# Scores of a token tile as one scheduled step, with the row halves of the TensorE array in turn, in a banded attention and PReLU feed-forward kernel

## The chip, the cores and the metric

The kernel runs on one core of one Trainium2 chip. The metric is the device time of one execution in microseconds (us). Before the change it is 951.26 us, the median of three runs (951.15 to 951.86).

The engines are named as in the profile. PE is TensorE (matmuls, and PEld its weight loads), DVE is VectorE, ACT is ScalarE, POOL is GpSimd. SP is SyncE, whose queue issues most of the transfers.

## The reference

Attention over a causal band of 64 positions, for 8 sequences of 576 tokens with 8 heads of 64 elements, and then a feed-forward layer on all 4608 tokens (512 to 2048 to 512):

```python
scores = scale * np.matmul(q, k.transpose(0, 1, 3, 2))
mask = (rel >= 0) & (rel < window)              # rel = query position - key position, window = 64
scores = np.where(mask, scores, -1000000000.0)
scores = scores - np.max(scores, axis=-1, keepdims=True)
attn = np.exp(scores)
attn = attn / (np.sum(attn, axis=-1, keepdims=True) + 1e-09)
x = np.matmul(attn, v)                          # heads side by side: (4608, 512)
...
h = x @ w_in
g = np.maximum(h, 0.0) + alpha * np.minimum(h, 0.0)
return (g @ w_out).astype(np.float32)
```

q, k and v are float32. The two weight matrices arrive in eight bytes per element, and the kernel turns each into two parts, a high and a low one, of the type fp32r. Every product of the feed-forward layer is a sum of three matmuls of such parts.

## The kernel before, in words

**Tiling.** There are 36 tiles of 128 tokens, in 9 blocks of four. For each tile `attend` does the attention; for each block and each of the 16 slices f of the hidden layer `cell` does both matmul groups of the feed-forward layer. `weights(c)` fetches and converts one of 32 pieces of weights: piece 2f is the w_in slice of f, piece 2f + 1 the w_out slice.

**One tile's attention.** A tile is two windows of 64 queries (u = 0 and 1), each of which sees 128 keys. q and k lie with the 64 head elements along the partitions: window 0 in partitions 0 to 63, window 1 in partitions 64 to 127. A score matmul therefore uses a 64 by 64 piece of the array: its rows are given by u, its columns by which of two heads (h) it is for. Four pairs of heads (e) by two heads are 8 matmuls per window, and the scores of one window fill one PSUM bank. Each float32 matmul is two records in the trace. Behind the scores come a mask on DVE (L344, one per pair of heads and window), the exponential on ACT (L350), the norm (DVE L361 and L362, POOL L366), a transpose of the weights of attention (on PE, L383, for the first eight tiles; on DVE, L404, for the others), the values on PE (L419), and the split of the result into xh and xl (L423, L426).

**One cell.** 12 matmuls into `h` (L450), two passes of PReLU on ACT and DVE (L456, L459), a split into high and low parts (ACT L464, POOL or DVE L468), and 12 matmuls onto the four output banks `o` (L483).

**What sets the order.** Nothing is ordered at run time: each engine has one queue and works through it in order. The order is made beforehand, by the list scheduler `Plan`. Every piece of work is a `step` with the engines that may run it, how long it holds the engine and how long until its result is there, the steps it comes `after` (their results are needed) or `behind` (their start is enough), and the buffers it takes and gives back. `order` picks, again and again, the step that can start first, and among those that can start within 0.12 us of it the one with the earliest deadline. `deadlines` works these out backwards from the `want` times. A buffer is a name of a place in SBUF or a PSUM bank; of several free places other than the banks 4 to 7, the one that came free last is taken. Banks 4 to 7 go under the name "bank"; 0 to 3 are called "o" and belong to the output sums, and the first two tiles use them for scores and transposes.

**The steps around the change.** In `attend` the loads of a tile are two steps on SP, each the k of one window and two transfers of q, and one step for both transfers of v. The scores are two steps on PE, each `after` the load step of its own window and the second `behind` the first:

```python
sc = step({PE: (0.55, 0.65)}, score, [loads[u]], scores or behind, take=[sbk] + [wb] * (u == 0),
          give=[qb, kb])
```

A step whose transfer moves data is planned to land 1.3 us after its issue plus the time of its bytes behind those planned earlier, plus 1.5 us; there is no limit to how many are under way in the plan. In the program itself the transfers use eight semaphores in turn. From the second block on, a tile's loads are `behind` an earlier cell of the block before, and its scores `behind` a later one.

Of the kernel before, what the change touches and what calls it, by code (L numbers as in the profile page):

```python
# [9 lines left out]
F32 = mybir.dt.float32  # L10
# [4 lines left out]
ALU = mybir.AluOpType  # L15
# [6 lines left out]

HOP = 0.06
LOOK = 0.12


class Buffer:
# [15 lines left out]
class Plan:  # L43
# [15 lines left out]
    def deadlines(self):  # L59
        left = {id(s): len(s.before) for s in self.steps}  # L60
        todo = [s for s in self.steps if not s.before]
        while todo:
            s = todo.pop()
            lat = min(x[1] for x in s.engines.values()) + (3.0 + s.moved if s.moved else 0.0)
            s.late = min([s.want] + [b.late - (lat + HOP if s in b.after else 0.0) for b in s.before])
            for a in s.after + s.behind:
                left[id(a)] -= 1
                if not left[id(a)]:
                    todo.append(a)

    def order(self):
        self.deadlines()
        free = {e: 0.0 for e in (PE, DVE, ACT, POOL, SP)}
        lanes = 0.0
        left = {id(s): len(s.after) + len(s.behind) for s in self.steps}
        ready = [s for s in self.steps if not left[id(s)]]
        done = []
        while ready:
            best = None
            picks = {}  # L80
            for s in ready:
                t0 = max([0.0] + [a.end + HOP for a in s.after] + [a.start + 0.01 for a in s.behind])
                wants = {}
                for b in s.take:
                    wants[b.kind] = wants.get(b.kind, 0) + 1
                for kind, n in wants.items():
                    have = sorted(self.stock[kind])
                    t0 = max(t0, have[n - 1][0] + HOP if len(have) >= n else math.inf)
                if t0 == math.inf:
                    continue  # L90
                for e, (hold, lat) in s.engines.items():
                    picks.setdefault(e, []).append((max(t0, free[e]), s, e))
# [5 lines left out]
                    best = cost, x  # L98
            assert best, [s.late for s in ready]
            (_, (t, s, e)) = best  # L100

            hold, lat = s.engines[e]
            s.start, s.engine = t, e
            free[e] = t + hold
            s.end = t + lat
            if s.moved:
                lanes = max(lanes, t + hold + 1.3) + s.moved
                s.end = lanes + 1.5
            for b in s.take:
                have = self.stock[b.kind]  # L110
                have.sort()
# [28 lines left out]
def banded_attention_then_prelu_ffn(  # L140
# [11 lines left out]
    nc = tc.nc  # L152
    P = 128
# [138 lines left out]
    def attend(t, by_pe, want, loads_behind=(), behind=()):  # L292
        d = st[t]
        early = t < 2
        qb, kb, vb, wb, pb = Buffer("q", 2), Buffer("k", 2), Buffer("v", 1), Buffer("w", 2 if by_pe else 1), Buffer("pt", 1)
        loads = []
        for u in range(2):
            def load(_, u=u):
                if u == 0:
                    d["q"] = room(qb, [P, NP, 2, W], F32, f"q_{t}")  # L300
                    d["k"] = room(kb, [P, NP, 2, 2, W], F32, f"k_{t}")
                r = slice(u * D, (u + 1) * D)
                nc.sync.dma_start(d["k"][r].rearrange("d e b h w -> d e (b h w)"),
                                  kT[:, :, 2 * t + u:2 * t + u + 2].rearrange("e d b h w -> d e (b h w)"))
                for h in range(2):
                    (nc.scalar if t == 0 else nc.sync).dma_start(
                        d["q"][r, :, h, :], qT[:, :, t, h, u * W:(u + 1) * W].rearrange("e d q -> d e q"))
            loads.append(step({SP: (0.7 if t == 0 else 1.9, 1.9)}, load, (), loads_behind if u == 0 else loads[:1],
                              take=[qb, kb] if u == 0 else [], moved=2.1))

        def load_v(_):
            d["v"] = room(vb, [P, NP, 2, P], F32, f"v_{t}")
            for u in range(2):
# [4 lines left out]
        sums, scores = [], []  # L318
        for u in range(2):
            sbk = Buffer("o" if early else "bank", NP)  # L320

            def score(_, u=u, sbk=sbk):
                if u == 0:
                    d["w"] = room(wb, [P, NH, KW], F32, f"w_{t}")
                    d["nm"] = sb.tile([P, NH], F32, tag=f"nm{t % 2}", name=f"nm_{t}")
                    d["sm"] = sb.tile([P, NH], F32, tag=f"sm{t % 2}", name=f"sm_{t}")
                    d["rc"] = sb.tile([P, NH], F32, tag=f"rc{t % 2}", name=f"rc_{t}")
                d["s", u] = s = bank(sbk, [P, NP, KW], F32, f"s_{t}_{u}")
                r = slice(u * D, (u + 1) * D)
                for e in range(NP):  # L330
                    for h in range(2):
                        nc.tensor.matmul(s[h * W:(h + 1) * W, e], d["q"][r, e, h, :], d["k"][r, e, :, h, :],  # L332
                                         start=True, stop=True)
# [3 lines left out]
            scores = [sc]  # L337
            some = []
            for e in range(NP):
                g = u * NP + e  # L340

                def mask(_, u=u, e=e, g=g):
                    m = masks[:, 1 if (t * P + u * W) % seq == 0 else 0, :]
                    nc.vector.tensor_tensor_reduce(  # L344
                        out=d["w"][:, g, :], in0=d["s", u][:, e], in1=m, op0=ALU.add, op1=ALU.min,
                        scale=-SCALE, scalar=3.0e38, accum_out=d["nm"][:, g:g + 1])
# [6 lines left out]
                m = step({DVE: (0.21, 0.37)}, mask, [sc], give=[sbk])  # L353
                some.append(step({ACT: (0.385, 0.58)}, soft, [m]))
            sums.append(some)

# [16 lines left out]
        if by_pe:  # L373
            for u in range(2):
# [238 lines left out]
```

## Time and profile before

| | |
|---|---|
| median of three runs | 951.26 us (951.15 to 951.86) |
| profiled execution, its own time | 950.47 us |
| its span, first to last instruction | 948.8 us |
| granted TensorE clock, mean | 0.997 |
| PE busy | 923.4 us (97%) |
| DVE, ACT, POOL busy | 450.7, 387.0, 312.2 us |
| score matmuls (L332) | 1152 records, 66.3 us |
| value matmuls (L419) | 1152 records, 43.1 us |
| moved by DMA | 74.41 MB |

Busy time of PE counts each matmul until its modelled end, and successive matmuls overlap; so how long a group holds PE is read from its start to the start of the group behind it. In the rows of the time order, the first column is the start in us from the start of the span, the second how long the group of like instructions lasted, xN how many there are, and what stands in brackets is how long the engine was idle before and who ended that.

### The profile page before, as it was taken

To read this page: it belongs to the slowest core of one execution; us is meant where nothing else is said; L and a number is where in the kernel's file an instruction comes from. 1 tells how busy PE (TensorE), PEld (TensorE's weight loads), DVE (VectorE), ACT (ScalarE), POOL (GpSimd) and SP (SyncE) were. 2 spreads that over 40 slices of the span, in tenths; PEclk is the share of its full clock that TensorE was granted. 3 is DMA by queue.
4 is the path that set the end of the run, shared out by engine and by line. 5 is a ranking of instruction groups with operands and counts; after the bars stand their busy time and mean duration, and the time that the engine had idled before them with its cause. 6 is when DMAs were issued, how large, how long until landed. Compare 5 with 4: busy or idle time off the path is not lost.

```text
span 948.8 us, 15478 instructions
## 1 busy us (share of the span) xinstructions
PE 923.4 (97%) x5872; PEld 748.5 (79%) x5872; DVE 450.7 (48%) x1310; ACT 387.0 (41%) x1025; POOL 312.2 (33%) x243
## 2 busy tenths in 40 slices
PE   5799999999999999999999999999999999999998
PEld 4578877888888888888888888888888888888886
DVE  2787995444444444445344534454444444441111
ACT  4777775333433333333433333342333343332222
POOL 2565675322222222222322322222222222232221
PEclk9999999999999999999999999999999999999999
DMA  9697665320432025201620151205220432001001
GB/s 202 163 234 183 178 198 124 87 57 1 101 92 55 23 57 132 56 23 34 156 56 23 35 128 51 56 19 136 58 56 1 92 98 57 23 1 45 1 1 44
DMA packets 96409, 74.41 MB, mean 78 GB/s; under 512 B 44624, under 2 KB 89680, under 8 KB 96336
## 3 DMA queue, kind: packets, MB, share of 16 engines
q1 hardware_dynamic: 93184, 73.16, 31.0%
q8 instruction: 46, 0.75, 0.3%
q10 hardware_dynamic: 3152, 0.27, 0.3%
q14 instruction: 27, 0.22, 0.1%
HBM read 63.97 MB, written 9.44 MB: 77 GB/s over the span
## 4 chain that ended last, share of the span: by engine, by line
PE 86%; issue 1%; DVE 1%; POOLq 0%; ACT 0%; POOL 0%; ACTq 0%
PE o L483 39%; PE h L450 38%; PE s L332 5%; PE av L419 3%; POOLq L609 0%; PE t L383 0%; DVE wout_l L275 0%; DVE g L459 0%; ACT g L456 0%; DVE two L239 0%; DVE os L519 0%; ACT gh L464 0%; DVE val L256 0%; DVE two L247 0%; DVE w L344 0%
## 5 line engine op out<-in xcount | busy, mean ns | idle before, releaser
L468 POOL TENSOR_TENSOR gl<-g,gh 128x512 fp32r<-128x512 f32 (+1 forms) x136 | 174.0, 1280 | 441.3 <-ACT gh L464 435.0
L459 DVE SCALAR_TENSOR_TENSOR g<-h,s_sb,g 128x512 f32<-128x512 f32 (+1 forms) x148 | 108.9, 736 | 287.0 <-ACT g L456 285.9
L483 PE MATMUL o<-wout_h,gh 128*128 128x512 f32 x576 | 230.1, 400 | 0.0
L483 PE MATMUL o<-wout_l,gh 128*128 128x512 f32 x576 | 226.8, 394 | 1.2 <-POOL wout_l L275 0.8
L456 ACT ACTIVATE g<-h,sa_sb 128x512 f32<-128x512 f32 (+1 forms) x148 | 100.1, 677 | 304.6 <-PE h L450 304.1
L450 PE MATMUL h<-xh,win_h 128*128 128x512 f32 (+1 forms) x592 | 160.9, 394 | 2.2 <-ACT pt L388 1.1
L404 DVE STREAM_TRANSPOSE pt<-w 32x256 f32<-32x256 f32 x336 | 146.5, 436 | 34.3 <-POOL w L366 30.1
L483 PE MATMUL o<-wout_h,gl 128*128 128x512 f32 x576 | 160.7, 392 | 0.4 <-POOL gl L468 0.4
L450 PE MATMUL h<-xl,win_h 128*128 128x512 f32 (+1 forms) x592 | 155.5, 384 | 0.0
L450 PE MATMUL h<-xh,win_l 128*128 128x512 f32 (+1 forms) x592 | 154.9, 383 | 0.0
L350 ACT ACTIVATE w<-w,nm 128x128 f32<-128x128 f32 x288 | 111.8, 390 | 84.7 <-DVE nm L344 84.6
L464 ACT CAST gh<-g 128x512 fp32r<-128x512 f32 (+1 forms) x148 | 90.2, 609 | 132.8 <-DVE g L459 132.7
L450 PEld LDWEIGHTS h<-xh,win_h 128*128 128x128 f32 x592 | 107.4, 189 | 28.9 <-issue 5.2
L483 PEld LDWEIGHTS o<-wout_h,gh 128*128 128x128 f32 x576 | 108.3, 188 | 25.1 <-issue 0.5
L483 PEld LDWEIGHTS o<-wout_h,gl 128*128 128x128 f32 x576 | 108.4, 188 | 24.9 <-POOL gl L468 1.3
L450 PEld LDWEIGHTS h<-xl,win_h 128*128 128x128 f32 x592 | 109.8, 188 | 22.8
L483 PEld LDWEIGHTS o<-wout_l,gh 128*128 128x128 f32 x576 | 108.5, 188 | 24.2 <-POOL wout_l L275 1.9
L450 PEld LDWEIGHTS h<-xh,win_l 128*128 128x128 f32 x592 | 109.6, 188 | 22.3
L366 POOL TENSOR_TENSOR w<-w,rc 128x1024 f32<-128x1024 f32 (+1 forms) x44 | 70.2, 1595 | 163.1 <-DVE rc L362 149.7
L344 DVE CUSTOM_DVE_ANT_0 w<-s,masks 128x128 f32<-128x128 f32 x288 | 64.5, 286 | 90.4 <-PE s L332 90.2
L332 PE MATMUL s<-k,q 64*64 64x128 f32 x1152 | 66.3, 288 | 9.0 <-DMA q<-qT 6.4
L332 PEld LDWEIGHTS s<-k,q 64*64 64x64 f32 x1152 | 55.0, 140 | 23.7 <-issue 15.7
(44 smaller groups left out, 484.6 us busy)
## 6 DMA issues: line engine op xcount, KB each, us to landing
k<-kT SPq DMA_DIRECT2D x72, 256.0 KB, 3.9
v<-vN SPq DMA_DIRECT2D x72, 256.0 KB, 4.1
out<-os SPq DMA_DIRECT2D x36, 256.0 KB, 3.4
q<-qT SPq DMA_DIRECT2D x140, 64.0 KB, 3.4
raw<-w_in SPq DMA_DIRECT2D x16, 512.0 KB, 5.4
raw<-w_out SPq DMA_DIRECT2D x16, 512.0 KB, 4.2
q<-qT ACTq DMA_DIRECT2D x4, 64.0 KB, 5.4
alpha_sb<-alpha ACTq DMA_DIRECT2D x1, 8.0 KB, 5.4
```

The source lines that it names most:

```text
L332: nc.tensor.matmul(s[h * W:(h + 1) * W, e], d["q"][r, e, h, :], d["k"][r, e, :, h, :], start=True, stop=True)
L344: nc.vector.tensor_tensor_reduce(out=d["w"][:, g, :], in0=d["s", u][:, e], in1=m, op0=ALU.add, op1=ALU.min, scale=-SCALE, scalar=3.0e38, a ...
L350: nc.scalar.activation(w, w, AF.Exp, scale=-1.0, bias=d["nm"][:, g:g + 1], accum_out=d["sm"][:, g:g + 1])
L366: nc.gpsimd.tensor_tensor(out=w, in0=w, in1=d["rc"][:, g].unsqueeze(2).broadcast_to(list(w.shape)), op=ALU.mult)
L404: nc.vector.transpose(d["pt"][ks, :, r], d["w"][r, :, ks])
L419: nc.tensor.matmul(av[r, e, u * W:(u + 1) * W], d["v"][:, e, u, r], d["pt"][:, u * NP + e, h * W:(h + 1) * W], start=True, stop=True)
L450: nc.tensor.matmul(ph[:, :nt], wt[:, c, fs], xt[:, c, xs], start=(k == 0), stop=(k == 3 * NP - 1))
L456: nc.scalar.activation(d["g"], d["h"][:, :nt], AF.Copy, scale=sa_sb[:, f:f + 1])
L459: nc.vector.scalar_tensor_tensor(out=d["g"], in0=d["h"][:, :nt], scalar=s_sb[:, f:f + 1], in1=d["g"], op0=ALU.mult, op1=ALU.max)
L464: nc.scalar.copy(d["gh"], d["g"])
L468: (nc.gpsimd if e == POOL else nc.vector).tensor_tensor(out=d["gl"], in0=d["g"], in1=d["gh"].bitcast(F32), op=ALU.subtract)
L483: nc.tensor.matmul(po[t][0], gt[:, i * P:(i + 1) * P], wt[:, f, :], start=(f == 0 and k == 0), stop=(f == NF - 1 and k == 2))
```

## The change

A tile's scores become one step of 16 matmuls. It takes two banks at once and goes through pairs of heads, heads and windows in this order, so that matmuls on rows 0 to 63 and on rows 64 to 127 alternate. It is `after` all loads of q and k of the tile. Every transfer of a tile is a step of its own: two of k, four of q, two of v. The plan's landing times are shorter, at most eight transfers are under way in it, and some hold times on PE are changed, with a factor of 1.9 for the first two tiles. The load of alpha is planned as a step on ACT, and the step that uses it has a later `want`. The matmuls, their operands, and the transfers are the same in number and size.

```diff
+FLIGHT = 8
...
-            lat = min(x[1] for x in s.engines.values()) + (3.0 + s.moved if s.moved else 0.0)
+            lat = min(x[1] for x in s.engines.values()) + (2.0 + s.moved if s.moved else 0.0)
...
-        lanes = 0.0
+        lanes, flying = 0.0, []
...
+                if s.moved and len(flying) >= FLIGHT:
+                    t0 = max(t0, flying[0])
...
+            while flying and flying[0] <= t:
+                heapq.heappop(flying)
...
             if s.moved:
-                lanes = max(lanes, t + hold + 1.3) + s.moved
-                s.end = lanes + 1.5
+                lanes = max(lanes, t + hold + 0.6) + s.moved
+                s.end = lanes + 1.2
+                heapq.heappush(flying, s.end)
...
-        qb, kb, vb, wb, pb = Buffer("q", 2), Buffer("k", 2), Buffer("v", 1), Buffer("w", 2 if by_pe else 1), Buffer("pt", 1)
-        loads = []
+        qb, kb, vb, wb, pb = Buffer("q", 1), Buffer("k", 1), Buffer("v", 1), Buffer("w", 2 if by_pe else 1), Buffer("pt", 1)
+        loads, first_load = [], []
...
-                for h in range(2):
-                    (nc.scalar if t == 0 else nc.sync).dma_start(
-                        d["q"][r, :, h, :], qT[:, :, t, h, u * W:(u + 1) * W].rearrange("e d q -> d e q"))
-            loads.append(step({SP: (0.7 if t == 0 else 1.9, 1.9)}, load, (), loads_behind if u == 0 else loads[:1],
-                              take=[qb, kb] if u == 0 else [], moved=2.1))
+            loads.append(step({SP: (0.62, 0.62)}, load_k, (), [*loads_behind, *loads[:1]],
+                              take=[kb] if u == 0 else [], moved=1.18))
+        for u, h in ((0, 0), (0, 1), (1, 0), (1, 1)):
+            def load_q(e, u=u, h=h):
...
+            first_load.append(step({ACT if t == 0 else SP: (0.64, 0.64)}, load_q, (), [*loads_behind, *first_load[:1]],
+                                   take=[qb] if u == h == 0 else [], moved=0.45))
+        loads += first_load
...
-        lv = step({SP: (1.25, 1.25)}, load_v, (), loads_behind, take=[vb], moved=2.4)
+            lv.append(step({SP: (0.62, 0.62)}, load_v, (), [*loads_behind, *lv[:1]], take=[vb] if u == 0 else [],
+                           moved=1.18))
...
+        banks = [Buffer("o" if early else "bank", NP) for _ in range(2)]
+
+        def score(_):
...
+            d["s"] = [bank(banks[u], [P, NP, KW], F32, f"s_{t}_{u}") for u in range(2)]
+            for e in range(NP):
+                for h in range(2):
+                    for u in range(2):
+                        r = slice(u * D, (u + 1) * D)
+                        nc.tensor.matmul(d["s"][u][h * W:(h + 1) * W, e], d["q"][r, e, h, :], d["k"][r, e, :, h, :],
+                                         start=True, stop=True)
+
+        cold = 1.0 + 0.9 * (t < 2)
+        sc = step({PE: (1.05 * cold, 1.15 * cold)}, score, loads, behind, take=[*banks, wb], give=[qb, kb])
...
-                r = slice(u * D, (u + 1) * D)
-                for e in range(NP):
-                    for h in range(2):
-                        nc.tensor.matmul(s[h * W:(h + 1) * W, e], d["q"][r, e, h, :], d["k"][r, e, :, h, :],
-                                         start=True, stop=True)
-
-            sc = step({PE: (0.55, 0.65)}, score, [loads[u]], scores or behind, take=[sbk] + [wb] * (u == 0),
-                      give=[qb, kb])
...
-                tr = step({PE: (0.6, 0.8)}, turn, [sc] + ready[-1:], take=[tb] + [pb] * (u == 0), give=[wb])
+                tr = step({PE: (0.37 * cold, 0.5 * cold)}, turn, [sc] + ready[-1:], take=[tb] + [pb] * (u == 0), give=[wb])
...
-        va = step({PE: (1.0, 1.15)}, value, [lv] + ready, take=[ab], give=[vb, pb])
+        va = step({PE: (1.08 * cold, 1.2 * cold)}, value, lv + ready, take=[ab], give=[vb, pb])
...
-    a0 = step({SP: (0.05, 0.05)}, load_alpha, moved=0.1)
-    alphas = step({DVE: (0.8, 0.8)}, signs, [a0], want=9.0)
+    a0 = step({ACT: (0.64, 0.64)}, load_alpha, moved=1.0)
+    alphas = step({DVE: (0.8, 0.8)}, signs, [a0], want=14.0)
```

More of the change, by code (lines that the diff above doesn't have):

```diff
@@ L294, in attend, with load_k @@
         early = t < 2
-        qb, kb, vb, wb, pb = Buffer("q", 2), Buffer("k", 2), Buffer("v", 1), Buffer("w", 2 if by_pe else 1), Buffer("pt", 1)
-        loads = []
+        qb, kb, vb, wb, pb = Buffer("q", 1), Buffer("k", 1), Buffer("v", 1), Buffer("w", 2 if by_pe else 1), Buffer("pt", 1)
+        loads, first_load = [], []
         for u in range(2):
-            def load(_, u=u):
+            def load_k(_, u=u):
                 if u == 0:
-                    d["q"] = room(qb, [P, NP, 2, W], F32, f"q_{t}")
                     d["k"] = room(kb, [P, NP, 2, 2, W], F32, f"k_{t}")
@@ L311, in load_v @@
-        def load_v(_):
-            d["v"] = room(vb, [P, NP, 2, P], F32, f"v_{t}")
-            for u in range(2):
+            loads.append(step({SP: (0.62, 0.62)}, load_k, (), [*loads_behind, *loads[:1]],
+                              take=[kb] if u == 0 else [], moved=1.18))
+        for u, h in ((0, 0), (0, 1), (1, 0), (1, 1)):
+            def load_q(e, u=u, h=h):
+                if u == h == 0:
+                    d["q"] = room(qb, [P, NP, 2, W], F32, f"q_{t}")
+                r = slice(u * D, (u + 1) * D)
+                (nc.scalar if e == ACT else nc.sync).dma_start(
+                    d["q"][r, :, h, :], qT[:, :, t, h, u * W:(u + 1) * W].rearrange("e d q -> d e q"))
+            first_load.append(step({ACT if t == 0 else SP: (0.64, 0.64)}, load_q, (), [*loads_behind, *first_load[:1]],
+                                   take=[qb] if u == h == 0 else [], moved=0.45))
@@ L314, in load_v @@
+        loads += first_load
+        lv = []
+        for u in range(2):
+            def load_v(_, u=u):
+                if u == 0:
+                    d["v"] = room(vb, [P, NP, 2, P], F32, f"v_{t}")
                 nc.sync.dma_start(d["v"][u * W:(u + 1) * W].rearrange("w c b d -> w c (b d)"),
                                   vN[:, :, 2 * t + u:2 * t + u + 2].rearrange("c w b d -> w c (b d)"))
-        lv = step({SP: (1.25, 1.25)}, load_v, (), loads_behind, take=[vb], moved=2.4)
-        sums, scores = [], []
@@ L319, in attend @@
-        for u in range(2):
[L320 to L328, printed above, removed]
-                r = slice(u * D, (u + 1) * D)
-                for e in range(NP):
-                    for h in range(2):
-                        nc.tensor.matmul(s[h * W:(h + 1) * W, e], d["q"][r, e, h, :], d["k"][r, e, :, h, :],
-                                         start=True, stop=True)
-            sc = step({PE: (0.55, 0.65)}, score, [loads[u]], scores or behind, take=[sbk] + [wb] * (u == 0),
-                      give=[qb, kb])
-            scores = [sc]
+            lv.append(step({SP: (0.62, 0.62)}, load_v, (), [*loads_behind, *lv[:1]], take=[vb] if u == 0 else [],
+                           moved=1.18))
@@ new lines, in attend @@
+        banks = [Buffer("o" if early else "bank", NP) for _ in range(2)]
+        def score(_):
+            d["w"] = room(wb, [P, NH, KW], F32, f"w_{t}")
+            for x in ("nm", "sm", "rc"):
+                d[x] = sb.tile([P, NH], F32, tag=f"{x}{t % 2}", name=f"{x}_{t}")
+            d["s"] = [bank(banks[u], [P, NP, KW], F32, f"s_{t}_{u}") for u in range(2)]
+            for e in range(NP):
+                for h in range(2):
+                    for u in range(2):
+                        r = slice(u * D, (u + 1) * D)
+                        nc.tensor.matmul(d["s"][u][h * W:(h + 1) * W, e], d["q"][r, e, h, :], d["k"][r, e, :, h, :],
+                                         start=True, stop=True)
@@ L338, in attend @@
+        cold = 1.0 + 0.9 * (t < 2)
+        sc = step({PE: (1.05 * cold, 1.15 * cold)}, score, loads, behind, take=[*banks, wb], give=[qb, kb])
+        sums = []
+        for u in range(2):
             some = []
@@ L344, in mask @@
                     nc.vector.tensor_tensor_reduce(
-                        out=d["w"][:, g, :], in0=d["s", u][:, e], in1=m, op0=ALU.add, op1=ALU.min,
+                        out=d["w"][:, g, :], in0=d["s"][u][:, e], in1=m, op0=ALU.add, op1=ALU.min,
                         scale=-SCALE, scalar=3.0e38, accum_out=d["nm"][:, g:g + 1])
@@ L351, in soft @@
                                          accum_out=d["sm"][:, g:g + 1])
-                m = step({DVE: (0.21, 0.37)}, mask, [sc], give=[sbk])
+                m = step({DVE: (0.21, 0.37)}, mask, [sc], give=[banks[u]])
                 some.append(step({ACT: (0.385, 0.58)}, soft, [m]))
```

## The prediction, written before the changed kernel was run

> **What bounds the kernel now.** I read the page first (busy time, then the chain of waits), then the busy time by stretch of the span, then the instructions of TensorE (PE) in order of time.
>
> ```profile
> span 948.8 us, 15478 instructions
> PE 923.4 (97%) x5872; PEld 748.5 (79%) x5872; DVE 450.7 (48%) x1310; ACT 387.0 (41%) x1025; POOL 312.2 (33%) x243
> ...
> PE o L483 39%; PE h L450 38%; PE s L332 5%; PE av L419 3%; POOLq L609 0%; PE t L383 0%; DVE wout_l L275 0%; DVE g L459 0%; ACT g L456 0%; DVE two L239 0%; DVE os L519 0%; ACT gh L464 0%; DVE val L256 0%; DVE two L247 0%; DVE w L344 0%
> ```
>
> The chain that ends last is PE's own queue; the scores of line 332 are 5% of it. A busy PE is not PE at its peak, so the next question is where it is idle. Columns: stretch, length, busy time and instructions of each engine, granted clock, DMA share, GB/s.
>
> ```profile
> 0.00:57.00 57.00, 37.64 (x350) 30.38 (x350) 32.11 (x115) 34.21 (x103) 27.28 (x34) 0.97 0.81 186
> 57.00:124.00 67.00, 65.34 (x432) 52.74 (x432) 57.06 (x129) 50.31 (x123) 42.82 (x34) 1.00 0.80 198
> 124.00:936.00 812.00, 811.93 (x5056) 659.09 (x5057) 359.40 (x1065) 299.96 (x797) 239.97 (x175) 1.00 0.24 61
> 936.00:949.00 13.00, 8.48 (x36) 6.31 (x34) 2.13 (x3) 2.48 (x4) 2.10 (x2) 0.94 0.21 81
> ...
> 100.00:124.00 24.00, 22.72 (x151) 17.93 (x149) 23.40 (x46) 19.18 (x44) 16.04 (x13) 1.00 0.77 204
> ```
>
> There are three regimes. From 124 to 936 us PE is never idle (811.93 of 812.00), while VectorE (DVE), ScalarE (ACT) and GpSimd (POOL) are under half busy: a microsecond taken off PE there comes off the end. From 57 to 124 us PE is idle for 1.66 us, but DVE, which converts the weights, is busy for 57.06 of 67 and for 23.40 of the last 24: PE and the weights are both close to the bound. Before 57 us PE is idle for 57.00 - 37.64 = 19.4 us; latencies set the time there.
>
> **The change, part 1: both row halves in turn.** Now a tile's scores are two steps of 8 matmuls, 16 records each: first all of array rows 0-63 (u = 0), then all of rows 64-127. Here is what a half costs alone, what both cost one behind the other, and what surrounds them.
>
> ```profile
> 66.04 1.09 PE L332 MATMUL s<-k,q 64*64 64x128 f32 x16
> 67.06 0.50 PE L483 MATMUL o<-wout_h,gh 128*128 128x512 f32 x1
> ...
> 389.89 1.07 PE L483 MATMUL o<-wout_h,gl 128*128 128x512 f32 x4
> 390.89 1.59 PE L332 MATMUL s<-k,q 64*64 64x128 f32 x32
> 392.41 1.21 PE L450 MATMUL h<-xh,win_h 128*128 128x512 f32 x4
> 393.46 1.09 PE L450 MATMUL h<-xl,win_h 128*128 128x512 f32 x4
> ...
> 398.05 1.07 PE L450 MATMUL h<-xh,win_h 128*128 128x512 f32 x4
> 398.96 1.07 PE L450 MATMUL h<-xl,win_h 128*128 128x512 f32 x4
> ...
> 406.33 1.15 PE L419 MATMUL av<-pt,v 128*64 128x64 f32 x32
> 407.41 0.50 PE L483 MATMUL o<-wout_h,gh 128*128 128x512 f32 x1
> ```
>
> Measured from start to the next group's start, one half alone holds PE for 67.06 - 66.04 = 1.02 us, and both for 392.41 - 390.89 = 1.52 us. The second half adds only 0.50 us, not 1.02: the two halves of the array already work at the same time for about half of a step. They don't overlap fully because the second half's instructions stand behind all 16 of the first in one queue. With the halves in turn both are fed from the start, and the array work is that of one half: 1.02 us is the lower bound. The other bound is how fast PE takes instructions: the value step (line 419) has the same 32 records and 32 weight loads and holds PE for 407.41 - 406.33 = 1.08 us, so issuing need not take longer than that; with a tail like that of a score, 1.15 us. I take 1.05, nearer to 1.02, since two halves that overlap are the same work as the half that was timed. The gain per tile is 1.52 - 1.05 = 0.47 us (bounds 0.37 and 0.50). Entering the 64-row form (1.00 instead of 0.91 us from the group ahead: 0.09) and leaving it (1.05 instead of 0.91 behind: 0.14) are paid once per step and stay.
>
> ```profile
> 57.00:124.00 67.00, 6.54 (x96) 5.09 (x96) 1.00 0.80 198
> 124.00:169.00 45.00, 2.18 (x32) 1.70 (x32) 1.00 0.60 162
> 169.00:936.00 767.00, 44.54 (x896) 37.77 (x896) 1.00 0.22 55
> ```
>
> These are the score matmuls alone by stretch: 896 records from 169 us on are 28 of the 36 tiles, and 44.54 / 28 = 1.59 us each, so all 28 have the form seen at 390.89. The gain there is 28 x 0.47 = **13.2 us** (10.4 to 14.0). No other engine takes it back: the next busiest, DVE, is at 359.40 of 812.
>
> One tile in the full stretch has its halves apart:
>
> ```profile
> 139.51 1.09 PE L332 MATMUL s<-k,q 64*64 64x128 f32 x16
> ...
> 143.51 1.09 PE L332 MATMUL s<-k,q 64*64 64x128 f32 x16
> ```
>
> It pays 2 x (1.02 + 0.09 + 0.14) = 2.50 and will pay 1.05 + 0.23 = 1.28: **1.2 us**. Three more tiles (the 96 records of the stretch from 57 to 124 us) have this form, the one at 66.04 among them: 3 x 1.2 = 3.7 us of PE work. Whether it shortens that stretch depends on the weights, since DVE was busy for 23.40 of the last 24 us. Bounds 0 and 3.7; with both engines as near to full I take the middle, **1.8 us**.
>
> [...]
>
> **Part 2: two banks together.** Now the second half may be planned into the very PSUM bank that the first half's masks are emptying. The trace shows that in the opening:
>
> ```profile
> 9.84 0.28 DVE L344 CUSTOM_DVE_ANT_0 w<-s,masks 128x128 f32<-128x128 f32 x1
> 10.23 1.97 PE L332 MATMUL s<-k,q 64*64 64x128 f32 x16 [1.20 <-issue]
> 17.02 2.89 PE L332 MATMUL s<-k,q 64*64 64x128 f32 x32
> 25.96 1.97 PE L332 MATMUL s<-k,q 64*64 64x128 f32 x16
> 28.98 0.29 DVE L344 CUSTOM_DVE_ANT_0 w<-s,masks 128x128 f32<-128x128 f32 x1
> 29.37 1.97 PE L332 MATMUL s<-k,q 64*64 64x128 f32 x16 [1.44 <-issue]
> 32.69 1.98 PE L419 MATMUL av<-pt,v 128*64 128x64 f32 x32 [1.34 <-issue]
> 36.76 0.72 PE L450 MATMUL h<-xh,win_h 128*128 128x256 f32 x4
> ```
>
> The second halves at 10.23 and 29.37 start just as the last mask of their first halves ends (10.12 and 29.27), although PE had been idle for 1.20 and 1.44 us. With a bank each, that wait is gone. A half takes 1.97 us in this slow opening, both one behind the other 2.89 less the overlap of their ends; in turn I expect some 2.0. The third tile's scores, now from 25.96 to 31.34, would end near 28, and the value step at 32.69, behind them in PE's queue and ahead of the first FFN cell at 36.76, could start up to 4 us earlier. Against that, the new step waits for all six loads of k and q, not for its half's: at tile 0 the masks start later than now, and its softmax is a chain on ACT that ends about when it does today (cost 0). If the weights are what comes next, the gain of 4 us turns into PE idling before line 483. Bounds: -3 (two more waits like the 1.44) and +4; I take the middle of zero and the gain, **2 us**.
>
> **Part 3: the planner's loads.** Each load becomes a step of its own, with landing costs cut and at most eight planned under way. The number and size of transfers don't change; alpha is planned on ACT, where it was issued before.
>
> ```profile
> 0.80 3.00 ACTq L306 DMA_DIRECT2D q<-qT  x4
> 3.83 0.62 ACTq L530 DMA_DIRECT2D alpha_sb<-alpha  x1
> ...
> 0.80 2.04 SPq L303 DMA_DIRECT2D k<-kT  x3
> 4.86 1.26 SPq L306 DMA_DIRECT2D q<-qT  x2
> ...
> SPq L306 <- DMA q<-qT: 2.0, 1, 2.0
> ...
> 392.52 0.59 SPq L303 DMA_DIRECT2D k<-kT  x1
> ...
> 415.85 1.59 PE L332 MATMUL s<-k,q 64*64 64x128 f32 x32
> ...
> 490.67 1.59 PE L332 MATMUL s<-k,q 64*64 64x128 f32 x32
> ```
>
> Eight transfers go out, and the ninth, at 4.86, waits for a landing: the program already has eight at most under way. The planner now knows it; no wait is added on the chip. What changes is the order on SyncE's queue (SP) in the opening, where weights, k, q and v share it; that is part of the -3 to +4 above. Later the loads are covered: the k of a later tile is issued at 392.52, as soon as a score frees its buffer, and even the next score, at 415.85, stands 23 us away. Without that cover a late load would cost its landing, some 4 us, once. The new hold times for transposes and values cost nothing by themselves; they alter the order only.
>
> **Sum.** 13.2 + 1.2 + 1.8 + 2 = 18.2 us. The profiled execution took 950.47 us (span 948.8 plus 1.7 around it); it would take 932.3. The median of the runs is 0.8 above it, so the forecast is 933.1 us.
>
> **Rivals.** (a) *The opening gives nothing*: the weights hold the first 124 us as they are. 951.3 - 14.4 = 937; if the new order loses 3 us there, 940. For it: DVE at 23.40 of 24. Against it: 19.4 us of PE idling before 57 us. (b) *The opening gives all*: 13.2 + 1.2 + 3.7 + 4 = 22 us, 929; with 1.02 us per score, 926. (c) *The halves in turn go no faster than one behind the other*, because the overlap needs a queue filled with one half: 1.52 us stays. Then only parts 2 and 3 and the four split tiles are left: 0 to 6 us, about 948. Against it: the overlap of 0.52 us seen in every tile needs nothing of the kind. (d) *Slower*: alternating makes the halves take turns, each switch between them waiting until the other's matmul is through. A step then costs up to 2 x 1.02 = 2.04 us, 0.52 more than now, times 28 = 14.6; less what the split tiles give, about 964. It decides as soon as a score takes over 1.52 us. Every overlap in the trace speaks against it; no row has the halves alternating.
>
> **How the numbers follow.** Forecast (931 to 936) 0.58; (a) 0.17; (b) 0.15; (c) 0.04; (d) 0.06. The range takes in (a) and (b) and leaves (c), (d) out: 926 to 942. About 0.2%, 1.9 us, is what a measurement of this kernel can tell from no change. Forecast, (a) and (b) are all faster by more; (c) is split between faster and the same: faster 0.91, same 0.03, slower 0.06.
>
> **What would show it.** Scores: one group of 32 records per tile, next group about 1.05 us behind (1.52 today); the score matmuls' busy time from 169 us on falls from 44.5 to about 31 us. PE is still full to within some 13 us of the end. The fourth score behind the one at 390.89 starts at 490.67, 99.8 us later; with 4 x 0.47 less this becomes 97.9. Part 2: no score group of 16 behind a PE wait, and a first FFN cell ahead of 36.76 us. The prediction is wrong if a score stays at 1.5 us, if PE shows idle time behind 140 us, or if the PE idling before 124 us grows by more than the 5 us that its work shrinks there.

## The result, and the profile after

The changed kernel takes 927.95 us (median of 4 runs, 927.52 to 929.16). The kernel before, run beside it, takes 951.2 us (948.08 to 951.86). The ratio is 0.9764, with a 95% interval of 0.9741 to 0.9787. The forecast was 933.1 us in a range of 926 to 942. The profiled execution of the changed kernel took 927.88 us.

From the page of the changed kernel: the span, the busy time of the engines, and the chain that ended last.

```profile
span 926.1 us, 15462 instructions
PE 898.2 (97%) x5872; PEld 727.8 (79%) x5872; DVE 448.0 (48%) x1312; ACT 385.1 (42%) x1024; POOL 311.3 (34%) x242
...
PE h L462 40%; PE o L495 39%; PE av L431 4%; PE s L343 3%; DMA raw<-w_in 2%; DMA raw<-w_out 1%; ACT w L362 1%; DMA alpha_sb<-alpha 1%; DVE val L261 1%; POOL val L265 1%; PE t L395 1%; ACT gh L476 0%; POOL w L378 0%; DVE g L471 0%; DVE w L356 0%
```

PE is still the chain, with the scores now at 3% of it (5% before). Here the chain is followed back to the first microseconds, through the transfers of weights into `raw` and the steps that convert them (`val`); before the change it breaks off at 119.96 us, so the two beginnings can't be compared. The same span by stretch, with the columns as in the prediction (busy time and instructions of PE, PEld, DVE, ACT, POOL):

```profile
0.00:57.00 57.00, 34.94 (x365) 28.49 (x366) 34.22 (x121) 35.80 (x107) 27.83 (x34) 0.85 0.81 190
57.00:124.00 67.00, 65.63 (x448) 52.86 (x447) 59.76 (x135) 52.78 (x127) 48.44 (x39) 1.00 0.83 211
124.00:914.00 790.00, 790.00 (x5033) 641.01 (x5032) 351.91 (x1055) 294.01 (x788) 233.74 (x170) 1.00 0.25 61
914.00:927.00 13.00, 7.65 (x32) 5.48 (x30) 2.13 (x3) 2.49 (x4) 1.27 (x1) 0.94 0.22 81
```

PE is full from 124 us to 12 us before the end, as before. Before 124 us it idles for 22.06 + 1.37 = 23.4 us, against 19.36 + 1.66 = 21.0 us before the change, and yet more PE instructions are through by then (813 against 782). The score matmuls of the last 28 tiles alone (PE, PEld), and a score in the order of time:

```profile
157.00:914.00 757.00, 30.91 (x896) 24.14 (x896) 1.00 0.23 57
```
```profile
222.39 1.15 PE L431 MATMUL av<-pt,v 128*64 128x64 f32 x32
223.47 1.10 PE L343 MATMUL s<-k,q 64*64 64x128 f32 x32
...
256.12 1.10 PE L343 MATMUL s<-k,q 64*64 64x128 f32 x32
257.15 1.21 PE L462 MATMUL h<-xh,win_h 128*128 128x512 f32 x4
```

A score now holds PE for 257.15 - 256.12 = 1.03 us, where it took 1.52. The 896 records of the last 28 tiles are busy for 30.91 us instead of 44.54.

**Where the 22.7 us of span went.** The four stores of a block's output stand together on SP's queue, so the start of such a group marks the end of a block. Here are those of the first block and of the eighth, before and after:

```profile
162.09 2.28 SPq L522 DMA_DIRECT2D out<-os  x4
...
859.43 1.80 SPq L522 DMA_DIRECT2D out<-os  x4
```
```profile
154.41 2.30 SPq L534 DMA_DIRECT2D out<-os  x4
...
836.52 1.80 SPq L534 DMA_DIRECT2D out<-os  x4
```

The first block ends 162.09 - 154.41 = 7.7 us earlier. The seven blocks from there took (859.43 - 162.09) / 7 = 99.62 us each and now take (836.52 - 154.41) / 7 = 97.44: 2.18 less, 15.2 us in all. Four scores per block at 0.49 us explain 1.96 of the 2.18. The rest of the span gives back 0.2.

Up to the first of these marks PE has the same 1026 records in both kernels (first row before, second row after, the columns as above):

```profile
0.00:162.09 162.09, 141.00 (x1026) 113.41 (x1027) 118.24 (x299) 109.53 (x278) 95.30 (x87) 0.99 0.74 182
0.00:154.41 154.41, 130.98 (x1026) 105.88 (x1027) 116.20 (x300) 108.40 (x277) 94.07 (x86) 0.94 0.77 191
```

So in the first block PE works 10.0 us less, of which the scores are 8.4 (21.77 us of busy time before, 13.35 now), and idles 2.3 us more (21.1 and 23.4).

### The profile page after: what moved, and what is told of

The parts are those of the page before. It is cut to its first block, busy times and chain, and to the rows that moved or that the text cites. A ratio compares the mean times of both kernels' runs of the same rounds, so it can differ in the third digit from the quotient of the medians.

```text
span 926.1 us, 15462 instructions
## 1 busy us (share of the span) xinstructions
PE 898.2 (97%) x5872; PEld 727.8 (79%) x5872; DVE 448.0 (48%) x1312; ACT 385.1 (42%) x1024; POOL 311.3 (34%) x242
## 4 chain that ended last, share of the span: by engine, by line
PE 86%; DMA 4%; ACT 3%; DVE 3%; issue 2%; POOL 1%; ACTq 0%; POOLq 0%; DVEq 0%; SPq 0%
PE h L462 40%; PE o L495 39%; PE av L431 4%; PE s L343 3%; DMA raw<-w_in 2%; DMA raw<-w_out 1%; ACT w L362 1%; DMA alpha_sb<-alpha 1%; DVE val L261 1%; POOL val L265 1%; PE t L395 1%; ACT gh L476 0%; POOL w L378 0%; DVE g L471 0%; DVE w L356 0%
## 5 line engine op out<-in xcount | busy, mean ns | idle before, releaser
L480 POOL TENSOR_TENSOR gl<-g,gh 128x512 fp32r<-128x512 f32 (+1 forms) x142 | 180.8, 1273 | 426.2 <-ACT gh L476 379.5
L495 PE MATMUL o<-wout_h,gh 128*128 128x512 f32 x576 | 227.6, 395 | 0.0
L362 ACT ACTIVATION_READ_ACCUMULATOR w<-w,nm 128x1 f32 x288 | 53.8, 187 | 0.0
L343 PE MATMUL s<-k,q 64*64 64x128 f32 x1152 | 44.3, 290 | 8.2 <-DMA k<-kT 5.4
```

What stands on the lines that cost most here:

```text
L343: nc.tensor.matmul(d["s"][u][h * W:(h + 1) * W, e], d["q"][r, e, h, :], d["k"][r, e, :, h, :], start=True, stop=True)
L480: (nc.gpsimd if e == POOL else nc.vector).tensor_tensor(out=d["gl"], in0=d["g"], in1=d["gh"].bitcast(F32), op=ALU.subtract)
L495: nc.tensor.matmul(po[t][0], gt[:, i * P:(i + 1) * P], wt[:, f, :], start=(f == 0 and k == 0), stop=(f == NF - 1 and k == 2))
```

## The experiments

### Halves one after the other, in the new plan

The plan, the loads and the two banks stay; the 16 matmuls of the step go through one window and then the other.

```diff
-            for e in range(NP):
-                for h in range(2):
-                    for u in range(2):
+            for u in range(2):
+                for e in range(NP):
+                    for h in range(2):
```

> The changed kernel with one edit: inside the score step the window is the outer loop again, so all matmuls on rows 0 to 63 stand ahead of those on rows 64 to 127. Plan, loads and banks are the same. My theory (the alternation makes the gain in the full stretch): a score holds TensorE for 1.52 us again instead of 1.03, 36 x 0.49 = 17.6 us more, so about 945 us. Rival (the gain comes from one step, two banks and the plan): 928 us, and a score of 1.03 us.

Measured: 941.79 us (941.02 to 942.97), ratio to before 0.9908 (0.9893 to 0.9923). First PE, then the ends of the first and eighth block:

```profile
257.60 1.59 PE L343 MATMUL s<-k,q 64*64 64x128 f32 x32
259.12 1.21 PE L462 MATMUL h<-xh,win_h 128*128 128x512 f32 x4
```
```profile
153.88 2.34 SPq L534 DMA_DIRECT2D out<-os  x4
...
849.68 1.80 SPq L534 DMA_DIRECT2D out<-os  x4
```

The score is back at 259.12 - 257.60 = 1.52 us, and the kernel is 13.8 us slower than the changed one: 28 x 0.49 = 13.7. So the alternation is worth that much, and only by the last 28 tiles (the expectation had counted all 36): with the slower scores the first block ends no later (153.88 against 154.41). Up to that mark PE works 5.3 us more than in the changed kernel (136.24 against 130.98) and idles 5.8 us less, so what the alternation saves there comes back as idle time. One thing more differs: up to 57 us the granted clock was 1.00 here and 0.85 in the changed kernel. A block takes (849.68 - 153.88) / 7 = 99.40 us, 0.22 less than before the change, with scores as slow as before; this is taken up in the experiment on the value step.

### The merged step alone, and the plan alone

One kernel puts a single alternating score step with two banks into the kernel before, with its loads and its plan. The other is the changed kernel with two score steps per tile, as before.

```diff
...
-            sc = step({PE: (0.55, 0.65)}, score, [loads[u]], scores or behind, take=[sbk] + [wb] * (u == 0),
-                      give=[qb, kb])
...
+        sc = step({PE: (1.05, 1.15)}, score, loads, behind, take=[*banks, wb], give=[qb, kb])
...
```
```diff
...
-        sc = step({PE: (1.05 * cold, 1.15 * cold)}, score, loads, behind, take=[*banks, wb], give=[qb, kb])
...
+            sc = step({PE: (0.55 * cold, 0.65 * cold)}, score, [loads[u], loads[2 + 2 * u], loads[3 + 2 * u]], scores or behind,
+                      take=[sbk] + [wb] * (u == 0), give=[qb, kb])
...
```

> The kernel before with the one alternating score step and its two banks, but with its loads, landing costs and hold times as they were. My theory: 28 x 0.49 = 13.7 us, the four tiles that had their halves apart 4.9 us, a value step directly ahead of a score eight times at 0.2 us: 951.2 - 20 = 931 us. Rival (the plan of the loads makes much of the gain): 938 us or more.

> The changed kernel with two score steps per tile as before, one for each window and after its own three loads; loads per transfer, eight under way, landing costs and hold times as changed. My theory: only what the opening gains is left, some 2.7 us: 948 us. Rival (the plan makes much of the gain): 940 us or less.

Measured: the merged step alone 933.69 us (932.88 to 934.24), ratio 0.982 (0.9804 to 0.9837); the plan alone 947.35 us (945.82 to 948.01), ratio 0.9959 (0.9944 to 0.9973). Block ends on SP's queue, first of the merged step alone, then of the plan alone:

```profile
160.40 2.96 SPq L520 DMA_DIRECT2D out<-os  x4
...
842.51 1.80 SPq L520 DMA_DIRECT2D out<-os  x4
```
```profile
159.54 2.38 SPq L536 DMA_DIRECT2D out<-os  x4
...
856.90 1.80 SPq L536 DMA_DIRECT2D out<-os  x4
```

The merged step alone has the whole gain per block, (842.51 - 160.40) / 7 = 97.44 us, and 1.7 of the 7.7 us of the first block. The plan alone has none per block (99.62 us) and 2.6 of the first. The first block's gain is not a sum: 1.7 and 2.6 apart, 7.7 together. (The expectation for the merged step had 4.9 us for four split tiles there.) With the merged step alone PE works 8.9 us less up to the mark (132.07), but idles 7.2 us more (28.3); with the plan alone it works 1.9 us less (139.06) and idles 0.6 us less (20.5). Only with both does most of the saved work shorten the block: 10.0 us less work, 2.3 us more idle time.

### How long a run of one half may be

Instead of changing the half at every matmul, it is changed after two, and after four. (The halves one after the other, above, are runs of eight.)

```diff
             for e in range(NP):
-                for h in range(2):
-                    for u in range(2):
+                for u in range(2):
+                    for h in range(2):
```
```diff
-            for e in range(NP):
-                for h in range(2):
-                    for u in range(2):
+            for e2 in range(0, NP, 2):
+                for u in range(2):
+                    for e, h in ((e2, 0), (e2, 1), (e2 + 1, 0), (e2 + 1, 1)):
```

> The changed kernel, with two matmuls of one half ahead of two of the other. My theory (a half can start as long as some three matmuls of the other stand ahead of it unissued, which is where the second half started before the change): a score stays at 1.03 to 1.06 us, 928 us. Rival (only strict alternation feeds both halves): 0.1 us more per score or above, 932 us.

> The changed kernel, with four matmuls of one half ahead of four of the other. My theory: the second half starts one matmul of 0.11 us late, so a score takes some 1.15 us, 0.12 x 36 = 4 us more: 932 us. Rival (strict alternation is needed): four matmuls late, some 1.4 us per score, 941 us.

Measured: runs of two 926.87 us (926.78 to 927.4), ratio 0.9746 (0.9729 to 0.9763); runs of four 927.68 us (927.27 to 929.53), ratio 0.9757 (0.974 to 0.9773). A score in the order of time, runs of two and then runs of four:

```profile
255.15 1.10 PE L343 MATMUL s<-k,q 64*64 64x128 f32 x32
256.19 1.21 PE L462 MATMUL h<-xh,win_h 128*128 128x512 f32 x4
```
```profile
255.75 1.15 PE L343 MATMUL s<-k,q 64*64 64x128 f32 x32
256.84 1.20 PE L462 MATMUL h<-xh,win_h 128*128 128x512 f32 x4
```

Runs of one, two, four and eight hold PE for 1.03, 1.04, 1.09 and 1.52 us. Runs of up to four are enough (1.15 us was expected for four), and by the total time the three can't be told apart. Behind the run of four the next two groups take 1.03 and 0.91 us instead of 1.05 and 0.93, so only some 0.02 of its 0.06 us is lost in the end.

The trace shows the overlap too, with modelled ends: counted in steps of 0.1 us from the start of a score, at most 8 score records are under way with one half alone (at 66.04 before the change) and 12 to 15 for most of the step with the halves in turn (at 256.12 in the changed kernel). In runs of eight (at 390.89 before the change) it is 8 from 0.3 us on, up to 14 in the middle and 6 towards the end. The times can be read as a second half that starts late when the run ahead of it is long: not at all for up to two matmuls, by 0.06 us for four, by 0.49 us for eight. The whole half takes 1.02 us for 8 matmuls, 0.13 each. So with runs of eight the second half starts about 0.49 / 0.13 = 3.8 matmuls late although 8 stand ahead of it. This is an estimate from these steps, not a view of the queue.

### The value step straight ahead of the next tile's score

In the changed kernel 8 of the 36 scores stand directly behind a value step (as at 222.39 and 223.47), in the kernel before none does. Here a value step waits in the plan for the place of the next tile's score, and both are taken together; 21 scores then stand so. What is planned first changes, the work does not.

```diff
...
-                x = min((x for x in some if x[0] <= first + LOOK), key=lambda x: (x[1].late, x[0]))
+                x = min((x for x in some if x[0] <= first + LOOK), key=lambda x: (x[1].late - x[1].rush, x[0]))
...
+        after_turn = [values[t - 1]] if t > 8 and t % NBLK else []
+        sc = step({PE: (1.05 * cold, 1.15 * cold)}, score, loads, [*behind, *after_turn], take=[*banks, wb], give=[qb, kb])
+        if after_turn:
+            sc.rush = 1e6
...
+        va = step({PE: (1.08 * cold, 1.2 * cold)}, value, lv + ready, turn_behind, take=[ab], give=[vb, pb])
+        values[t] = va
+        if turn_behind:
+            va.rush = 1e6
...
+                g = {0: 4, 1: 8, 2: 11}.get(i)
+                st_done[t] = attend(t, n == 1, at(n - 1, f) + 24.0, [first[n - 1, max(0, f - 3)]], [first[n - 1, f]],
+                                    [first[n - 1, g]] if n > 1 and g else [])
```

> The changed kernel with a plan in which, from the third block on, a tile's value step waits for the cell at which the next tile's scores are due and both are taken one directly behind the other, 21 times instead of 8. My theory (entering and leaving the 64-row form costs 0.23 us unless a step with half-array matmuls stands beside it): 13 x 0.23 = 3.0 us less than the changed kernel, 925 us. Rival (the switch is paid by each of the two steps whatever stands beside): 928 us; if the later value step holds up the next block, more.

Measured: 924.4 us (923.57 to 925.59), ratio 0.9725 (0.9711 to 0.974): the fastest kernel of this study. PE in the order of time, and the block ends on SP's queue:

```profile
270.18 1.15 PE L436 MATMUL av<-pt,v 128*64 128x64 f32 x32
271.26 1.10 PE L345 MATMUL s<-k,q 64*64 64x128 f32 x32
272.29 0.50 PE L503 MATMUL o<-wout_h,gh 128*128 128x512 f32 x1
```
```profile
153.75 2.61 SPq L542 DMA_DIRECT2D out<-os  x4
...
832.50 1.80 SPq L542 DMA_DIRECT2D out<-os  x4
```

The two steps take 1.08 and 1.03 us, no more than each does by itself; but PE enters and leaves the small forms once for both instead of twice. A block takes (832.50 - 153.75) / 7 = 96.96 us, 0.48 less than the changed kernel. With 13 more such pairs in the seven blocks this is 7 x 0.48 / 13 = 0.26 us a pair, and the prediction's rows give 0.09 + 0.14 = 0.23 us for entering and leaving. The changed kernel gained about one pair per block without meaning to, as did the halves one after the other: this fits the 0.22 us per block that the latter still saved.

### The plan's limit of eight, and its landing costs

One kernel lifts the limit; the other restores the landing costs.

```diff
-FLIGHT = 8
+FLIGHT = 99
```
```diff
-            lat = min(x[1] for x in s.engines.values()) + (2.0 + s.moved if s.moved else 0.0)
+            lat = min(x[1] for x in s.engines.values()) + (3.0 + s.moved if s.moved else 0.0)
...
-                lanes = max(lanes, t + hold + 0.6) + s.moved
-                s.end = lanes + 1.2
+                lanes = max(lanes, t + hold + 1.3) + s.moved
+                s.end = lanes + 1.5
```

> The changed kernel with the plan's limit of transfers under way at 99 instead of 8; on the chip the eight semaphores stay. My theory (what the plan knows of the loads matters in the opening alone): within 2 us of 928. Rival (the limit in the plan keeps late loads out of the way of early ones): 932 us or more.

> The changed kernel with the landing costs of the plan before (3.0 in the deadlines, 1.3 and 1.5 in the order). My theory: within 2 us of 928, as only the opening depends on them. Rival (shorter landing costs make the opening's gain): 931 us or more.

Measured: without the limit 927.42 us (925.03 to 929.29), ratio 0.9749 (0.9727 to 0.9771); with the old landing costs 928.48 us (928.39 to 929.17), ratio 0.9763 (0.9748 to 0.9777). Neither can be told from the changed kernel. So neither is what moves the first block.

### What moves the end of the first block

The last of the 32 pieces of weights becomes ready with this step on DVE, before and after:

```profile
154.28 1.10 DVE L275 TENSOR_TENSOR wout_l<-val,wout_h 128x512 fp32r<-128x512 f32 x1 [1.47 <-ACT wout_h L271]
```
```profile
146.57 1.11 DVE L280 TENSOR_TENSOR wout_l<-val,wout_h 128x512 fp32r<-128x512 f32 x1 [1.49 <-ACT wout_h L276]
```

It ends at 155.38 and 147.68, 7.7 us apart like the stores, which follow 6.7 us behind it in both. In eleven of the fourteen kernels of this study the stores follow the last piece by 6.5 to 7.3 us (in the others by 5.4, 7.5 and 10.4). PE doesn't idle for this piece: it is ready 0.3 us ahead of its first use in both, and the plan has filled the time before with other work. The weights are also early at the start: the fourth fetch is issued 7.6 us earlier (SP's queue, before and after), since in the new plan the first piece is joined ahead of the second tile's masks.

```profile
26.34 0.54 SPq L228 DMA_DIRECT2D raw<-w_in  x1
```
```profile
18.76 0.37 SPq L233 DMA_DIRECT2D raw<-w_in  x1
```

Four kernels test whether that beginning is the cause. The first holds the conversion of the first four pieces on DVE back in the changed kernel, behind the masks of tile 1:

```diff
                 m = step({DVE: (0.21, 0.37)}, mask, [sc], give=[banks[u]])
+                if t == 1:
+                    for x in first_dve:
+                        x.behind.append(m)
+                        m.before.append(x)
...
+        if c < 4:
+            first_dve.extend((s2, s4))
```

> The changed kernel with one constraint more in its plan: VectorE takes up the first four pieces of weights only behind the masks of the second tile, as the kernel before does. My theory now (the opening's 7.6 us come from the first piece of weights being converted while VectorE would wait for the second tile's scores, so that its raw buffer is free and the next fetch goes out 7 us earlier): the first block ends near 162 us instead of 156, 5 to 6 us more than the changed kernel, 933 us. Rival (the merged step and its two banks make the opening's gain): 928 us.

Measured: 931.31 us (929.45 to 931.4), ratio 0.9784 (0.9768 to 0.9801), 3.4 us above the changed kernel. Its DVE, SP and PE rows:

```profile
148.33 1.35 DVE L281 TENSOR_TENSOR wout_l<-val,wout_h 128x512 fp32r<-128x512 f32 x1 [1.21 <-ACT wout_h L277]
```
```profile
25.68 0.54 SPq L234 DMA_DIRECT2D raw<-w_in  x1
...
156.21 2.35 SPq L541 DMA_DIRECT2D out<-os  x4
```
```profile
33.39 1.22 PE L469 MATMUL h<-xh,win_h 128*128 128x256 f32 x4
```

The profiled execution took 929.45 us, so its rows show only part of the 3.4 us: the last piece is ready at 149.68, 2.0 us later than in the changed kernel, and the store is 1.8 us later. The block was expected to end near 162 us; of the 6.9 us by which the fourth fetch is later (25.68 against 18.76), only 2.0 reach the last piece. Attention was helped by this: the first cell starts at 33.39 us, 4 us earlier than in the changed kernel. It didn't shorten the block. Its end moved with the weights, not with the first cell.

The second and the third kernel do the reverse to the merged step alone and to the plan alone: the masks of tile 1 stand behind the join of the first piece.

```diff
...
-                m = step({DVE: (0.21, 0.37)}, mask, [sc], give=[banks[u]])
+                m = step({DVE: (0.21, 0.37)}, mask, [sc], [cv[0]["join"]] if t == 1 else [], give=[banks[u]])
```

> The run with the scores alone changed (old plan of the loads, 933.7 us), and the second tile's masks planned behind the first piece's join on VectorE. My theory: if the early first piece is enough, the first block ends near 156 us instead of 162 and the time is 928 us. Rival (it needs the early fetch of the fourth piece too, which this plan still puts behind the loads of the fourth tile): 932 to 934 us.

> The run with the plan alone changed (two score steps, 947.4 us), and the second tile's masks planned behind the first piece's join on VectorE; the planner then also fetches that piece ahead of the second tile's k. My theory: 942 us, the first block ending near 156 us instead of 161. Rival (order on VectorE is not what holds the opening): 947 us.

Measured: 933.62 us (931.78 to 934.1), ratio 0.981 (0.9793 to 0.9827), and 948.78 us (948.56 to 952.16), ratio 0.9984 (0.9971 to 0.9998). Neither is faster than without the edit (933.69 and 947.35). In both the first piece came earlier and the fourth fetch did not (25.4 and 27.4 us). An early first piece alone is not the cause.

The fourth takes the fastest kernel and puts the loads of tile 1 behind the fetch of the first piece:

```diff
...
-                st_done[t] = attend(t, True, EARLY[i])
+                st_done[t] = attend(t, True, EARLY[i], [cv[0]["fetch"]] if t == 1 else [])
```

> The run with the value step directly ahead of the next scores (924.4 us), and the second tile's loads planned behind the fetch of the first piece of weights. My theory (the weights hold the first block): the first piece is ready some 3 us earlier and the first block ends 1 to 3 us earlier, 922 us. Rival (the second tile's attention, some 3 us later, holds it): 925 us or more.

Measured: 925.83 us (924.66 to 926.07), ratio 0.9729 (0.9714 to 0.9744), against 924.4 (923.57 to 925.59) without it: no faster. DVE and SP:

```profile
143.59 1.59 DVE L281 TENSOR_TENSOR wout_l<-val,wout_h 128x512 fp32r<-128x512 f32 x1 [1.49 <-ACT wout_h L277]
```
```profile
155.60 2.36 SPq L542 DMA_DIRECT2D out<-os  x4
```

In the profiled execution the last piece is ready at 145.18, 1.9 us earlier than in the kernel it was made from (147.06), and the block ends 1.9 us later (155.60 against 153.75). The stores follow 10.4 us behind the weights instead of 6.7. What holds them is not shown. In line with the rival, PE's waits for the norm of attention grow from 8.8 to 10.8 us in the first 160 us; but POOL, which does that norm and a part of the weights, is also busy for longer up to the mark (103.9 us against 94.3). An early last piece alone doesn't end the block earlier.

## Why the prediction was right, and where it was not

**The scores: right.** The step "I take 1.05" measured 1.03 us, and 28 x 0.49 = 13.7 us stand where the sum had 13.2. The cause is the one given, as the halves one after the other show: the same plan without the alternation loses 13.8 us. Rivals (c) and (d) are out: a score takes neither 1.52 nor 2.04 us.

These times don't fit matmuls that start strictly in the order of the queue. Runs of eight take 1.52 us, less than the 2 x 1.02 that two halves would need one behind the other. Runs of four speak more clearly: if no matmul could start ahead of one before it in the queue, each run would start at least three matmuls of 0.13 us behind the run before it, and the four runs would take some 3 x 0.39 + 4 x 0.13 = 1.7 us, by an estimate from 1.02 / 8. They take 1.09. From one group to the next the order of the queue does hold: the 1859 groups of like matmuls on PE before the change, and the 1856 after it, start in the order of the program.

**The first block: right in sign, undersized, and by reasons that did not hold as given.** The sum had 1.2 + 1.8 + 2 = 5.0 us for it and 7.7 came. That the two are as near as this is luck. Two of its steps don't stand as given:

- "It pays 2.50 and will pay 1.28: 1.2 us", and the 1.8 us of the three other split tiles, counted PE time in the first block as time. PE did get the saving (8.4 us of busy time in the scores there), but PE time by itself is not what the block's length follows: with the halves one after the other eight tiles have slower scores, and the block ends 0.5 us earlier; with the merged step alone 7.2 of 8.9 us come back as idle time. The merged step has a part in the gain all the same: without it the changed plan ends the block 5.1 us later (159.54 against 154.41). Whether by PE time or by the order of the other engines was not taken apart. The forecast had read the warning (DVE busy for 23.40 of 24 us) and split the difference.
- That the value step at 32.69 "could start up to 4 us earlier" did not come true, as PE shows in the opening of the changed kernel:

```profile
9.51 1.96 PE L343 MATMUL s<-k,q 64*64 64x128 f32 x26 [1.27 <-DMA q<-qT]
17.87 1.99 PE L343 MATMUL s<-k,q 64*64 64x128 f32 x32
...
27.42 1.99 PE L343 MATMUL s<-k,q 64*64 64x128 f32 x32
32.42 1.98 PE L431 MATMUL av<-pt,v 128*64 128x64 f32 x32 [3.01 <-DVE val L261]
...
37.39 1.20 PE L462 MATMUL h<-xh,win_h 128*128 128x256 f32 x4
38.39 1.05 PE L462 MATMUL h<-xl,win_h 128*128 128x256 f32 x4
...
40.23 1.66 PE L343 MATMUL s<-k,q 64*64 64x128 f32 x32
41.82 0.73 PE L462 MATMUL h<-xh,win_h 128*128 128x256 f32 x4
```

The third score does end near 29.4 instead of 31.34, and a score costs the 2.0 us expected. But the value step idles for 3.01 us and starts at 32.42; the profile names the join of a piece of weights on DVE as what it waited for. The step doesn't read that piece. By the order that `Plan` works out for this kernel it takes the PSUM bank that this join gives back, while another of the four had not been used yet. The first cell starts at 37.39, not ahead of 36.76. What moved with the block's end, by the same 7.7 us, is the last piece of weights. The prediction noted that the order on SP's queue changes in the opening and priced it at -3 to +4 us within the opening alone; it never asked what an earlier conversion of the first pieces does to the last.

**The second banks** did what the diff says: the waits of the prediction's rows for the first half's masks are gone, and no group of 16 stands behind a PE wait. Apart from the first loads, what PE waits for in the opening is now mainly the norm and a join of weights (columns: us in total, times, longest):

```profile
PE t L395 <- POOL w L378: 8.0, 4, 3.5
...
PE av L431 <- DVE val L261: 4.0, 2, 3.0
```

**Rivals (a) and (b).** The time lies in the span of (b), 926 to 929, but not by its sum, which had 4 us from an earlier first cell: this cell starts 0.6 us later. (The 926 doesn't follow from that sum either: 1.02 us per score instead of 1.05 takes 0.8 us off 929.) The premise of (a), that the weights hold the first 124 us, fits the runs; its conclusion, that they stay as they are, did not hold. The idle time of PE before 124 us grew by 2.4 us, which is under the 5 that the prediction named as a sign of being wrong.

**Not foreseen at all:** the value steps directly ahead of a score, 7 x 0.22 = 1.5 us. The prediction had the price (0.09 and 0.14, "paid once per step and stay") and didn't ask whether two such steps could share it.

By the ends of the blocks the account closes: 18.2 + 0.5 (scores) + 1.5 (pairs) + 2.7 (first block) - 0.2 (end) = 22.7 us.

**What stays open.** Holding the first four pieces back costs 3.4 us by the medians; starting the first piece earlier brings none by itself. What else in the new plan makes 7.7 us out of 1.7 and 2.6 was not settled: the merged step, the separate loads and the hold times change the planner's order together, and they were not all taken apart.

## What to carry to other kernels

When a matmul uses only half of the array's rows, alternate the halves in the queue, in runs of at most four float32 matmuls (here 1.03 to 1.09 us a score, against 1.52 with one half after the other), each half with a PSUM bank of its own (planned into one bank, two second halves started here only as the masks of their first halves ended, with PE idle for 1.20 and 1.44 us), and put steps that use a part of the array side by side, so that entering and leaving that form is paid once (here 0.26 us a pair). Price a saving on an engine only in the stretch where that engine is full: here the same 0.49 us counted in 28 tiles and not in the first eight. Where a planner decides the order, look for what a changed cost or a merged step does to the longest chain of another resource, here the weights, before pricing the step itself.

## What the runs showed of the hardware

**The other half's matmuls are reached across a short run.** Runs of one, two, four and eight matmuls per half cost 1.03, 1.04, 1.09 and 1.52 us per 16 matmuls, against 1.02 us for 8 of one half alone: in runs of one or two the second half costs 0.01 to 0.02 us.

**Two spells at half the clock.** Four matmuls of 128 by 256 into `h` take 1.05 us at 38.39 in the changed kernel and 0.73 us at 41.82; before the change they took 0.72 us at 36.76 already. The granted clock by stretch, before and after:

```profile
30.00:40.00 10.00, 7.98 (x98) 6.72 (x94) 5.24 (x18) 6.69 (x19) 5.03 (x4) 1.00 0.59 183
```
```profile
30.00:40.00 10.00, 6.44 (x52) 5.88 (x52) 6.52 (x26) 6.09 (x21) 3.72 (x3) 0.50 0.66 194
```

PE has fewer instructions in this stretch after the change (52 against 98), is busy for less of it (6.44 us against 7.98), and is granted half the clock. The kernel before has such a spell later: PE works for 0.11 us between 46 and 48 us, the clock is 0.50 between 50 and 52, and the same four matmuls take 1.06 us at 51.80. Clock and durations don't agree everywhere: before the change the value step at 32.69 took 1.98 us, as long as after, in a stretch granted 1.00. Nor does little work on PE always come with a low clock: in the first 10 us it is busy for 2.65 us before and 1.83 after, and is granted 1.00 in both. No run changes the clock alone, so neither what lowers it nor what it cost here is shown.

**Two small forms side by side share their entry and exit:** 0.26 us per pair of a value step and a score, by the block period (96.96 us with 13 more pairs in seven blocks, against 97.44).
